# Attention keys in three chunks of 128 and a rest of 64, the rests of two head pairs on four quarters of the array

One core of one Trainium2 chip. The metric is the device time of one execution in microseconds (us). TensorE, VectorE, ScalarE and GpSimd are PE, DVE, ACT and POOL in the lines of the profile; PEld is the weight load of TensorE.

## The reference

```python
batch, n_heads, seq, head_dim = (8, 12, 448, 64)      # all fp32
def rmsnorm(x, g):
    return x / np.sqrt(np.mean(x * x, axis=-1, keepdims=True) + 1e-06) * g
q_n, k_n = rmsnorm(q, g_q), rmsnorm(k, g_k)
scores = (1 / sqrt(64)) * q_n @ k_n.T                  # per head, 448 x 448
attn = exp(scores - max) / (sum + 1e-9)
x = attn @ v                                           # to (3584, 768)
# then a SwiGLU feed-forward: rmsnorm(x), 768 -> 1536 (gate, value) -> 768
```

## The kernel before

Heads go in 48 pairs, six to a sequence. The 448 keys of a head are four chunks of 112. Per head pair: q and k are squared (ScalarE), reduced (VectorE) and turned into 1/rms (GpSimd power), q is multiplied by it (GpSimd), both are transposed on TensorE (`turn`) and copied out of PSUM. Scores have the keys on the output's partitions, so that k's 1/rms is the scale of the exp. Values and the sums of the exps accumulate over the chunks, a reciprocal follows, then the product x. While `direct(g)` holds (the first seven pairs) the sums are matmuls of ones over all exps; later GpSimd adds the exps first. In between run the matmuls of the feed-forward of the sequence before (`fill`). Up to about 300 us VectorE, ScalarE and GpSimd also convert the weights that arrive by DMA (`convert`).

```python
    ps_s, ps_m, ps_f = pool("c_ps_s", 4, space=PSUM), pool("c_ps_m", 1, space=PSUM), pool("c_ps_f", 3, space=PSUM)
    ...
    def turn(g, i):
        ...
        ps = (ps_m if todo else ps_f).tile([128, 512], F32, name="tr", tag="m" if todo else "f")
        for t in range(NT):                               # NT = 4, P = 112
            nc.tensor.transpose(ps[:, t * P:(t + 1) * P], src[:, t * 2 * D:(t + 1) * 2 * D], ident[0:P, 0:P])
        dst, flat = st["qkT", g][:, i, :], ps[:, 0:S]
        if i == 0:
            nc.scalar.activation(dst, flat, ACT.Copy, scale=gqk[:, 0:1])
        else:
            nc.vector.tensor_copy(dst, flat)

    def score(g, cs):
        ...
        for c in cs:
            for j in range(2):                            # j: head of the pair
                r = slice(j * D, (j + 1) * D)
                ps = sc[c, j] = ps_s.tile([128, 512], F32, name="sc", tag="s")
                nc.tensor.matmul(ps[0:P, 0:S], lhsT=qkT[r, 1, c * P:(c + 1) * P], rhs=qkT[r, 0, :], start=True, stop=True)
        ...                                               # exps; then add(): GpSimd, two adds after chunks 0 and 1, four after 2 and 3

    def values(g):
        vt = st["v", g]
        av = st["av", g] = ps_m.tile([128, 512], F32, name="av", tag="m")
        for c in range(NT):
            for j in range(2):
                nc.tensor.matmul(av[j * D:(j + 1) * D, 0:S], lhsT=vt[:, j, c, :], rhs=st["e", g, c, j],
                                 start=(c == 0), stop=(c == NT - 1))

    def sums(g):
        ...                                               # den: ones x exps
        rd = tmp.tile([128, S], F32, name="rd", tag="rd", bufs=1)
        if direct(g):
            nc.vector.reciprocal(rd, den[:, 0:S])
        ...
        nc.vector.tensor_tensor(x, av[:, 0:S], rd, ALU.mult)
        ...
            after(1 if soon else 3, lambda: nc.scalar.activation(rd, x, ACT.Square))
            after(1 if soon else 4, lambda: (nc.gpsimd.tensor_tensor(ss, ss, rd, ALU.add), ...))
    ...
        if g <= NPAIR:                                    # one head pair of the first stage (convert() cut)
            pe(lambda: score(g, (0, 1)))
            pe(lambda: turn(g + 1, 0)); pe(lambda: turn(g + 1, 1))
            pe(lambda: values(g - 1))
            pe(lambda: sums(g - 1))
            pe(lambda: score(g, (2, 3)))
```

Line numbers in the profiles are those of each kernel's own source. In the kernel before, scores are L476, values L501, sums L512, transposes L461; in the changed kernel scores are L532, values L579, sums L592, transposes L515 and L518, the quarters L556 (scores), L562 (values) and L567 (sums).

Of the kernel before, what the change touches and what calls it, by code (L numbers as in the profile page):

```python
# [20 lines left out]
NT, P = 4, 112  # L21
NPAIR = H // 2
# [312 lines left out]
def safe_scores(  # L335
# [28 lines left out]
    e_pool, tmp, y_pool = pool("c_e", 12), pool("c_tmp", 1), pool("c_y", 2)  # L364
# [25 lines left out]

    def load_pair(g):
        if g >= NG:
            return
        b, hp = divmod(g, NPAIR)
        hs = slice(2 * hp, 2 * hp + 2)
        qk = st["qk", g] = qk_pool.tile([P, 2, 2 * NT * D], F32, name="qk")
        nc.sync.dma_start(out=qk[:, 0].rearrange("p (h n) -> p h n", h=2), in_=q[b, hs].rearrange("h (p t) d -> p h (t d)", t=NT))

        for h in range(2):
            nc.sync.dma_start(out=qk[:, 1].rearrange("p (t h d) -> p h t d", h=2, d=D)[:, h],  # L400
                              in_=k[b, 2 * hp + h].rearrange("(p t) d -> p t d", t=NT))

    def load_v(g):
        if g >= NG:
            return
        b, hp = divmod(g, NPAIR)
        vt = st["v", g] = v_pool.tile([P, 2, NT, D], F32, name="vt")
        nc.sync.dma_start(out=vt.rearrange("p h t d -> p h (t d)"),
                          in_=v[b, 2 * hp:2 * hp + 2].rearrange("h (p t) d -> p h (t d)", t=NT))
# [5 lines left out]
    def squares(g, i):  # L415

        if g >= NG:
            return
        n = 2 * NT
        if i == 0:  # L420
            st["ms", g] = small.tile([P, 2 * n], F32, name="ms")
        ms = st["ms", g]
        sq = tmp.tile([P, n * D], F32, name="sq", tag="sq", bufs=2)
        nc.scalar.activation(sq, st["qk", g][:, i], ACT.Square)  # L424

        def reduce():
            nc.vector.tensor_reduce(out=ms[:, i * n:(i + 1) * n], in_=sq.rearrange("p (n d) -> p n d", d=D), axis=AX_X, op=ALU.add)  # L427

        after(1, reduce)
        if g <= 1:  # L430

            after(1, lambda: rms_qk(g, slice(i * n, (i + 1) * n)))
            if i == 0:
                after(1, lambda: norm_q(g))
        elif i == 1:
            after(2, lambda: rms_qk(g))
            after(2, lambda: norm_q(g))

    def rms_qk(g, cols=slice(0, 4 * NT)):
        ms = st["ms", g][:, cols]  # L440
        nc.gpsimd.tensor_scalar(ms, ms, 1.0 / D, 1e-6, ALU.mult, ALU.add)
        if ("rs", g) not in st:
            st["rs", g] = small.tile([P, 4 * NT], F32, name="rs")
        nc.gpsimd.tensor_tensor(st["rs", g][:, cols], ms, mhalf[0:P, cols], ALU.pow)  # L444

    def norm_q(g):
        qn = st["qn", g] = qn_pool.tile([P, 2 * NT * D], F32, name="qn")
        nc.gpsimd.tensor_tensor(
            qn.rearrange("p (t h d) -> p h t d", h=2, d=D), st["qk", g][:, 0].rearrange("p (h t d) -> p h t d", h=2, d=D),
            st["rs", g][:, 0:2 * NT].rearrange("p (h t) -> p h t", h=2).unsqueeze(3).to_broadcast([P, 2, NT, D]), ALU.mult)  # L450

    def turn(g, i):

        if g >= NG:
            return
        if ("qkT", g) not in st:
            st["qkT", g] = qkT_pool.tile([128, 2, S], F32, name="qkT")
        src = st.pop(("qn", g)) if i == 0 else st["qk", g][:, 1]
        ps = (ps_m if todo else ps_f).tile([128, 512], F32, name="tr", tag="m" if todo else "f")
        for t in range(NT):  # L460
            nc.tensor.transpose(ps[:, t * P:(t + 1) * P], src[:, t * 2 * D:(t + 1) * 2 * D], ident[0:P, 0:P])  # L461
        dst, flat = st["qkT", g][:, i, :], ps[:, 0:S]
        if i == 0:
            nc.scalar.activation(dst, flat, ACT.Copy, scale=gqk[:, 0:1])
        else:
            nc.vector.tensor_copy(dst, flat)  # L466

    def score(g, cs):

        qkT, rs = st["qkT", g], st["rs", g]  # L470
        sc = {}
        for c in cs:
            for j in range(2):
                r = slice(j * D, (j + 1) * D)
                ps = sc[c, j] = ps_s.tile([128, 512], F32, name="sc", tag="s")
                nc.tensor.matmul(ps[0:P, 0:S], lhsT=qkT[r, 1, c * P:(c + 1) * P], rhs=qkT[r, 0, :], start=True, stop=True)  # L476
        for (c, j), ps in sc.items():
            e = st["e", g, c, j] = e_pool.tile([P, S], F32, name="e")
            n = 2 * NT + c * 2 + j
            nc.scalar.activation(e, ps[0:P, 0:S], ACT.Exp, scale=rs[:, n:n + 1])  # L480

        def add():
            for j in range(2):
                if cs[0] == 0:
                    es = st["es", g, j] = tmp.tile([P, S], F32, name="es", tag="es", bufs=4)
                    nc.gpsimd.tensor_tensor(es, st["e", g, 0, j], st["e", g, 1, j], ALU.add)  # L486
                else:
                    es = st["es", g, j]
                    for c in cs:
                        nc.gpsimd.tensor_tensor(es, es, st["e", g, c, j], ALU.add)  # L490

        if not direct(g):
            after(4 if g == NPAIR + 1 else 1, add)

    def values(g):

        vt = st["v", g]
        av = st["av", g] = ps_m.tile([128, 512], F32, name="av", tag="m")
        for c in range(NT):
            for j in range(2):  # L500
                nc.tensor.matmul(av[j * D:(j + 1) * D, 0:S], lhsT=vt[:, j, c, :], rhs=st["e", g, c, j],  # L501
                                 start=(c == 0), stop=(c == NT - 1))

    def sums(g):
# [3 lines left out]
        den = (ps_f if direct(g) else ps_s).tile([128, 512], F32, name="den", tag="f" if direct(g) else "s")  # L508
        terms = [[st["e", g, c, j] for j in range(2)] for c in range(NT)] if direct(g) else [[st["es", g, j] for j in range(2)]]
        for i, pair in enumerate(terms):  # L510
            for j, term in enumerate(pair):
                nc.tensor.matmul(den[j * D:(j + 1) * D, 0:S], lhsT=ones[0:P, :], rhs=term,  # L512
                                 start=(i == 0), stop=(i == len(terms) - 1))
# [20 lines left out]
        for c in range(NT):  # L534
            for j in range(2):
                st.pop(("e", g, c, j))
# [370 lines left out]
    def store(b, n, i, y):  # L907
        row0 = at = b * S + i * 128 - 64 * (b % 2)
        while at < row0 + 128:
            seq, col = divmod(at, S)  # L910
            t, p = divmod(col, P)
            m = min(P - p, row0 + 128 - at)
            rows = out[seq * S:(seq + 1) * S, n * HALF:(n + 1) * HALF].rearrange("(p t) n -> t p n", t=NT)[t, p:p + m, :]
            nc.sync.dma_start(out=rows, in_=y[at - row0:at - row0 + m, :])
            at += m
# [175 lines left out]
    for g in range(2):  # L1091
        load_pair(g)
# [6 lines left out]
    mhalf = const.tile([128, 4 * NT], F32, name="mhalf")  # L1099
# [3 lines left out]
    for a in range(2):  # L1103
        rows = slice(a * D, (a + 1) * D)
        nc.scalar.dma_start(out=gq[rows, :], in_=g_q.rearrange("(p o) -> p o", o=1))
        nc.scalar.dma_start(out=gk[rows, :], in_=g_k.rearrange("(p o) -> p o", o=1))
    load_v(0)
    load_pair(2)
# [26 lines left out]


    squares(0, 0)
    warm(9)
# [7 lines left out]
    pe(lambda: turn(0, 0))  # L1146
    squares(2, 0)
    squares(2, 1)
    for g in range(NG + 1):
        b, hp = divmod(g, NPAIR)  # L1150
        if g:
            load_pair(g + 3)
        if g == 0:
            pe(lambda: score(0, (0, 1)))
            pe(lambda: score(0, (2, 3)))
# [9 lines left out]
        if g <= NPAIR:  # L1165
            pe(lambda: score(g, (0, 1)))
            squares(g + 2, 0)
            squares(g + 2, 1)
            convert()
            if g == 1:  # L1170
                pe(lambda: values(0))
            pe(lambda: turn(g + 1, 0))
            pe(lambda: turn(g + 1, 1))
            if g > 1:
                pe(lambda: values(g - 1))
            load_v(g + 2)
            convert()
            pe(lambda: sums(g - 1))
            pe(lambda: score(g, (2, 3)))
            convert()  # L1180
            if g == 2:
                bound()
            continue

        if g < NG:
            pe(lambda: score(g, (0, 1)))
        pe(lambda: values(g - 1))
        load_v(g + 2)
        if g == NPAIR + 1:
            pe(lambda: rms_x(0))  # L1190
            pe(lambda: score(g, (2, 3)))
# [4 lines left out]
        elif g < NG:  # L1196
            pe(lambda: score(g, (2, 3)))
        if hp:
# [3 lines left out]
            pe(lambda: turn(g + 1, 0))  # L1202
            fill()
# [55 lines left out]
```

## Time and profile before

| kernel before | |
|---|---|
| time, median of 3 runs | 1626.95 us (1626.43 to 1628.05) |
| span of the profiled execution, mean granted clock | 1625.3 us, 0.999 |
| TensorE busy | 99% |
| VectorE, ScalarE, GpSimd busy | 54%, 31%, 39% |

Busy shares are means over 1625 us.

### The profile page before, as it was taken

What the parts mean: (1) busy time and instruction counts of PE and PEld (TensorE: products, weight loads), DVE (VectorE), ACT (ScalarE), POOL (GpSimd) and SP (SyncE); (2) the same over time, 40 slices, a digit from 0 to 9 for tenths busy, and PEclk for the clock granted to TensorE, in tenths of its full rate; (3) what the DMA queues carried; (4) which work ended last, traced back from release to release, by engine and by line L of the source; (5) the groups of instructions that cost most, each with busy time, mean ns of one, the idle gap of its engine ahead of it and who ended that gap; (6) DMA issues with size and microseconds to landing.
All of it is one profiled execution on the core that took longest, in us unless ns stands there. A gap on an engine that the chain in (4) does not pass through costs nothing.

```text
span 1625.3 us, 21571 instructions
## 1 busy us (share of the span) xinstructions
PE 1608.9 (99%) x7376; PEld 1139.7 (70%) x7376; DVE 871.2 (54%) x1425; ACT 500.3 (31%) x975; POOL 632.2 (39%) x569
## 2 busy tenths in 40 slices
PE   8999999999999999999999999999999999999998
PEld 4444445678855888568865788658786588969974
DVE  6989898487842555335572354624565234433431
ACT  7856563232222332232232222322332123100110
POOL 7777776343523434244334323434343223100000
PEclk9999999999999999999999999999999999999999
DMA  8756674666855555565544655466454453557651
GB/s 223 208 176 200 183 219 134 217 222 200 267 183 154 164 154 156 166 197 154 155 120 131 201 155 147 120 215 194 130 163 132 147 176 108 152 182 239 175 148 45
DMA packets 249036, 276.83 MB, mean 170 GB/s; under 512 B 66644, under 2 KB 245844, under 8 KB 248916
## 3 DMA queue, kind: packets, MB, share of 16 engines
q1 hardware_dynamic: 248596, 275.34, 56.7%
q8 instruction: 61, 1.00, 0.3%
q14 instruction: 59, 0.48, 0.1%
q10 hardware_dynamic: 320, 0.00, 0.0%
HBM read 235.93 MB, written 39.32 MB: 169 GB/s over the span
## 4 chain that ended last, share of the span: by engine, by line
PE 91%; DVE 5%; DMA 2%; ACT 1%; issue 0%; POOL 0%; SPq 0%; DVEq 0%; ACTq 0%; POOLq 0%
PE ff L797 41%; PE ff L991 21%; PE sc L476 9%; PE av L501 9%; PE den L512 3%; PE ff L892 3%; PE ff L1022 2%; PE tr L461 2%; DVE top L646 1%; DVE top L645 1%; DVE rd L520 1%; DVE top L644 1%; DMA raw<-in_moe_w_out_dram 0%; ACT e L480 0%; PE rb L558 0%; DMA raw<-in_moe_w_val_dram 0%
## 5 line engine op out<-in xcount | busy, mean ns | idle before, releaser
L797 PE MATMUL ff<-x,w 128*128 128x224 f32 x1770 | 359.3, 353 | 0.8 <-DVE u L809 0.8
L797 PEld LDWEIGHTS ff<-x,w 128*128 128x128 f32 x1770 | 332.2, 190 | 9.8 <-issue 6.7
L797 PE MATMUL ff<-xs,w 128*128 128x224 f32 x1326 | 272.3, 353 | 0.4 <-DVE cc L809 0.4
L480 ACT ACTIVATE e<-sc,rs 112x448 f32<-112x448 f32 x384 | 212.1, 638 | 190.2 <-PE sc L476 185.2
L486 POOL TENSOR_TENSOR es<-e 112x448 f32<-112x448 f32 x82 | 95.3, 1184 | 436.1 <-ACT e L480 436.0
L797 PEld LDWEIGHTS ff<-xs,w 128*128 128x128 f32 x1326 | 248.6, 190 | 6.1 <-issue 5.3
L490 POOL TENSOR_TENSOR es<-es,e 112x448 f32<-112x448 f32 x164 | 185.9, 1144 | 85.4 <-ACT e L480 78.9
L991 PE MATMUL ff<-w,h 128*128 128x384 f32 x600 | 203.4, 488 | 0.0
L520 DVE RECIPROCAL rd<-rd 128x448 f32<-128x448 f32 x41 | 121.1, 2953 | 135.9 <-ACT rd L519 135.9
L476 PE MATMUL sc<-qkT 64*112 64x448 f32 x768 | 176.7, 562 | 1.6 <-DVE qkT L466 0.8
L991 PEld LDWEIGHTS ff<-w,h 128*128 128x128 f32 x600 | 112.3, 190 | 78.6 <-issue 4.7
L501 PE MATMUL av<-e,vt 112*64 112x448 f32 x768 | 154.9, 545 | 0.0
L444 POOL TENSOR_TENSOR rs<-ms,mhalf 112x16 f32<-112x16 f32 (+1 forms) x50 | 143.7, 2874 | 4.2
L476 PEld LDWEIGHTS sc<-qkT 64*112 64x112 f32 x768 | 68.8, 172 | 93.2 <-issue 69.5
L991 PE MATMUL ff<-w,so 128*128 128x384 f32 x338 | 116.7, 488 | 2.0 <-DVE y L952 2.0
L501 PEld LDWEIGHTS av<-e,vt 112*64 112x64 f32 x768 | 50.8, 136 | 95.8 <-issue 73.9
L1022 PE MATMUL ff<-x,w 128*128 128x448 f32 x288 | 112.0, 542 | 0.0
L809 DVE TENSOR_TENSOR cc<-ff,u 128x448 f32<-128x448 f32 x84 | 52.3, 623 | 93.3 <-PE ff L797 93.0
L991 PEld LDWEIGHTS ff<-w,so 128*128 128x128 f32 x338 | 63.2, 190 | 46.5 <-DVE y L952 3.9
L427 DVE TENSOR_REDUCE ms<-sq 112x8 f32<-112x512 f32 x96 | 61.3, 678 | 52.0 <-ACT sq L424 51.7
L682 POOL TENSOR_TENSOR w<-top,raw 128x384 int32<-128x384 int32 x72 | 78.0, 1097 | 28.3 <-DVE top L646 13.4
L1022 PEld LDWEIGHTS ff<-x,w 128*128 128x128 f32 x288 | 53.3, 190 | 50.9 <-issue 49.0
(104 smaller groups left out, 1676.2 us busy)
## 6 DMA issues: line engine op xcount, KB each, us to landing
w<-kept SPq DMA_DIRECT2D x480, 192.0 KB, 3.2
w<-kept_o SPq DMA_DIRECT2D x290, 192.0 KB, 2.8
kept<-w SPq DMA_DIRECT2D x94, 192.0 KB, 3.7
top<-kept SPq DMA_DIRECT2D x72, 192.0 KB, 3.0
qk<-in_q_dram SPq DMA_DIRECT2D x48, 224.0 KB, 3.6
qk<-in_k_dram SPq DMA_DIRECT2D x96, 112.0 KB, 3.5
vt<-in_v_dram SPq DMA_DIRECT2D x48, 224.0 KB, 2.8
raw<-in_moe_w_gate_dram SPq DMA_DIRECT2D x24, 384.0 KB, 4.7
```

The source lines that it names most:

```text
L427: nc.vector.tensor_reduce(out=ms[:, i * n:(i + 1) * n], in_=sq.rearrange("p (n d) -> p n d", d=D), axis=AX_X, op=ALU.add)
L444: nc.gpsimd.tensor_tensor(st["rs", g][:, cols], ms, mhalf[0:P, cols], ALU.pow)
L476: nc.tensor.matmul(ps[0:P, 0:S], lhsT=qkT[r, 1, c * P:(c + 1) * P], rhs=qkT[r, 0, :], start=True, stop=True)
L480: nc.scalar.activation(e, ps[0:P, 0:S], ACT.Exp, scale=rs[:, n:n + 1])
L486: nc.gpsimd.tensor_tensor(es, st["e", g, 0, j], st["e", g, 1, j], ALU.add)
L490: nc.gpsimd.tensor_tensor(es, es, st["e", g, c, j], ALU.add)
L501: nc.tensor.matmul(av[j * D:(j + 1) * D, 0:S], lhsT=vt[:, j, c, :], rhs=st["e", g, c, j], start=(c == 0), stop=(c == NT - 1))
L520: nc.vector.reciprocal(rd, rd)
L682: nc.gpsimd.tensor_tensor(data(key).bitcast(I32), top, lo, ALU.add)
L797: nc.tensor.matmul(bank[:, w * HT:(w + 1) * HT], lhsT=wt[:, c * 128:(c + 1) * 128], rhs=x[:, c, :], start=onto is None and w == c == 0, st ...
L991: nc.tensor.matmul(ps, lhsT=a, rhs=data(("wo", b, name, c)), start=first and c == 0, stop=c == NFP - 1, skip_group_check=True)
L1022: nc.tensor.matmul(bank[w][:, 0:S], lhsT=data(key)[:, c * 128:(c + 1) * 128], rhs=st["x", 0, half][:, c, :], start=half == c == 0, stop=ha ...
```

## The change

The intent: four chunks of 112 rows use only 112 of the array's 128 rows or columns. Three chunks of 128 and a rest of 64 have less to do: the rest scores of two heads need 64 x 64 of the array each, and so do the rest values, so all four can stand on the four quarters at once. The rests of a sequence's six pairs are loaded, normalized and (q with k) transposed together. The core of the diff:

```diff
+    def norm_rests(b, lo, hi):
+        nc.scalar.activation(sq, rest, ACT.Square)
+        after(1, lambda: nc.vector.tensor_reduce(out=ms, in_=sq, axis=AX_X, op=ALU.add))
+        def rms():
+            nc.gpsimd.tensor_scalar(ms, ms, 1.0 / D, 1e-6, ALU.mult, ALU.add)
+            nc.gpsimd.tensor_tensor(rq, ms[0:D], half[0:D], ALU.pow)
+            nc.gpsimd.tensor_tensor(rest[0:D], rest[0:D], rq.unsqueeze(3).to_broadcast([D, n, 2, D]), ALU.mult)
+            for place in range(2):
+                nc.gpsimd.tensor_tensor(st["rr", b][own(place), lo:hi], ms[own(1), :, place], half[own(1), :, place], ALU.pow)
...
     def turn(g, i):
-        for t in range(NT):
-            nc.tensor.transpose(ps[:, t * P:(t + 1) * P], ...)
+        for t in range(NK):                                   # NK = 3
+            nc.tensor.transpose(ps[:, t * 128:(t + 1) * 128], ...)
         if i == 0:
+            nc.tensor.transpose(ps[:, NK * 128:], st["rest", b][:, hp].rearrange("p h d -> p (h d)"), ident)
+            nc.scalar.activation(dst[:, 0, :], ps[:, 0:S], ACT.Copy, scale=gqk[:, 0:1])
+            nc.vector.tensor_copy(dst[:, 1, LAST], ps[:, S:])
         else:
-            nc.vector.tensor_copy(dst, flat)
+            nc.vector.tensor_copy(dst[:, 1, FULL], ps[:, FULL])
...
         def add():                                            # once per pair, after the last chunk
+                nc.gpsimd.tensor_tensor(es, st["e", g, 0, j], st["e", g, 1, j], ALU.add)
+                nc.gpsimd.tensor_tensor(es, es, st["e", g, 2, j], ALU.add)
+                nc.gpsimd.tensor_tensor(es[r], es[r], rest[r], ALU.add)
...
+    def rests(g):                       # quarters: this pair's rest scores, the last pair's rest values (and sums)
+            for r in (own(0), own(1)):
+                nc.tensor.matmul(ps[r, 0:S], lhsT=qkT[r, 1, LAST], rhs=qkT[r, 0, :], start=True, stop=True)
+            for j in range(2):
+                nc.tensor.matmul(av[own(j), 0:S], lhsT=vr[across(j)], rhs=e[across(j)], start=True, stop=False, ...)
...
         if g <= NPAIR:
-            pe(lambda: score(g, (0, 1)))
-            pe(lambda: turn(g + 1, 0)); pe(lambda: turn(g + 1, 1))
-            pe(lambda: values(g - 1)); pe(lambda: sums(g - 1)); pe(lambda: score(g, (2, 3)))
+            pe(lambda: score(g, (0,)))
+            pe(lambda: turn(g + 1, 0)); some_rests(g); pe(lambda: turn(g + 1, 1))
+            pe(lambda: rests(g)); pe(lambda: values(g - 1))
+            pe(lambda: score(g, (1,))); pe(lambda: sums(g - 1)); pe(lambda: score(g, (2,)))
```

(In the later stages, `rests(g)` stands ahead of the first scores.)

## The prediction

> **What bounds the kernel now.** I read the page's busy shares first, then the costliest groups, then the timeline of one head pair in the long middle stage, and last the windows of the first 300 us.
>
> ```profile
> PE 1608.9 (99%) x7376; PEld 1139.7 (70%) x7376; DVE 871.2 (54%) x1425; ACT 500.3 (31%) x975; POOL 632.2 (39%) x569
> PE 91%; DVE 5%; DMA 2%; ACT 1%; issue 0%; POOL 0%; SPq 0%; DVEq 0%; ACTq 0%; POOLq 0%
> L476 PE MATMUL sc<-qkT 64*112 64x448 f32 x768 | 176.7, 562 | 1.6 <-DVE qkT L466 0.8
> L501 PE MATMUL av<-e,vt 112*64 112x448 f32 x768 | 154.9, 545 | 0.0
> ```
>
> TensorE is never idle to speak of, and the chain that ended last is TensorE for 91% of the span. So time comes only from fewer TensorE steps, and only where TensorE really holds the pace. Scores (L476) and values (L501) are a fifth of it. Each has 768 records for 48 x 8 = 384 matmuls: an fp32 matmul leaves two records. The timeline of TensorE around one pair of heads:
>
> ```profile
> 619.86 2.43 PE L797 MATMUL ff<-xs,w 128*128 128x224 f32 x12
> 622.23 1.76 PE L476 MATMUL sc<-qkT 64*112 64x448 f32 x8
> 623.92 3.23 PE L501 MATMUL av<-e,vt 112*64 112x448 f32 x16
> 626.98 0.92 PE L512 MATMUL den<-es,ones 112*64 112x448 f32 x4
> 627.83 1.78 PE L476 MATMUL sc<-qkT 64*112 64x448 f32 x8
> 629.54 2.54 PE L797 MATMUL ff<-x,w 128*128 128x224 f32 x12
> ```
>
> Take differences of starts, because the ends are modelled. Values: 626.98 - 623.92 = 3.06 us for 16 records, 0.191 each. A full-array matmul of the same 448 columns needs twice that:
>
> ```profile
> 122.11 7.03 PE L1022 MATMUL ff<-x,w 128*128 128x448 f32 x18
> 128.98 0.55 PE L461 MATMUL tr<-ident,qn 112*128 112x112 f32 x4
> ```
>
> (128.98 - 122.11) / 18 = 0.38 us. So the two heads' matmuls run side by side, on two halves of the array, and what counts is the number of **pair steps**: two records per matmul, 0.375 us apart, 0.75 us per pair. The weight loads show the 0.375 directly, two at a time:
>
> ```profile
> 622.70 0.18 PEld L476 LDWEIGHTS sc<-qkT 64*112 64x112 f32 x2 [0.20 <-issue]
> 623.07 0.18 PEld L476 LDWEIGHTS sc<-qkT 64*112 64x112 f32 x2 [0.20 <-issue]
> ```
>
> A head pair is then 2 + 4 + 1 + 2 = 9 pair steps = 6.75 us. It took 629.54 - 622.23 = 7.31 us; the 0.56 over falls on three stretches (1.69 - 1.50 = 0.19, 3.91 - 3.75 = 0.16, 1.71 - 1.50 = 0.21): each switch between halves by rows (scores), halves by columns (values, sums) and the whole array costs about 0.19 us.
>
> The first stage is another case:
>
> ```profile
> 36.40:47.70 11.30, 11.30 (x58) 4.68 (x58) 10.79 (x17) 9.06 (x18) 5.97 (x8) 1.00 0.76 222
> 59.00:70.30 11.30, 11.30 (x60) 4.68 (x58) 11.06 (x15) 9.05 (x18) 8.50 (x8) 1.00 0.73 214
> 150.00:200.00 50.00, 48.59 (x160) 23.41 (x158) 45.42 (x63) 25.52 (x53) 37.81 (x34) 1.00 0.61 181
> ```
>
> The columns are stretch and length, then busy time of TensorE, weight loads, VectorE, ScalarE, GpSimd. VectorE, which converts the weights, is 95 to 98% busy up to 82 us and 91% at 150 to 200 us, and GpSimd is at 53 to 76%. What TensorE saves there can turn into waiting.
>
> **What the Trainium skill says.** "TensorEngine Tiling (Array Packing)", Key Properties: tiles work independently, each with its own weight loads and matmuls, but "Changing tiling mode (not just tile) drains the TensorE". The trace agrees with both: pairs at 0.375 us a step, and 0.16 to 0.21 us lost per switch. "TensorE: Matmul & The Clock Gate", Part 3 (Packing small matmuls): a packed group spans one matmul plus about 4 ns per tile, measured there up to 16 tiles in bf16. Here the second of a pair starts 7 ns after the first; no group of four runs in this kernel, so four is carried over. The same page, LDWEIGHTS: a load's time goes with its columns, not its rows. The trace agrees (scores 64x112 about 172 ns, values 112x64 about 137 ns), so filling 128 partitions rather than 112 costs the values nothing. "PSUM — Partial Sum Buffer", collisions: it quotes that different row tiles are not able to write one bank at the same time. The trace of before cannot test that, since its row halves write different banks.
>
> **The change part by part.**
>
> *Removed:* per head pair, of the four pair steps of scores and of values one each (4 chunks of 112 become 3 of 128). Minus 1.50 us.
>
> *Added:* one group of four quarter matmuls: this head pair's two rest scores (rows and columns of the same half) and the last pair's two rest values (crossed). If four run as two did: 0.75 us. The heads lie crossed in the tiles for just this.
>
> *Switches:* before: scores, values + sums, scores: three stretches. After: quarters, scores, values + sums, scores: four. Plus 0.19 us.
>
> *Sum after the first stage:* 1 + 1 + 3 + 1 + 2 = 8 pair steps, 6.00 us, plus 0.75 of switches = 6.75 against 7.31: **minus 0.56 us per head pair**.
>
> *Transposes:* 8 of 112 columns become 7 of 128, the rests of q and k of a pair in one. Four took 613.04 - 612.65 = 0.39 us in the middle stage, 0.097 each; by columns 0.11 each, so 7 x 0.11 = 0.77 against 0.78. Nothing.
>
> *Sums while direct* (first seven head pairs): four pair steps stay four, since the rests' sums sit on quarters that the rest values already hold and queue behind them. There too it is 12 steps to 11.
>
> *ScalarE:* exps per pair 8 to 7. ScalarE is 31% busy and gives nothing, except in the first stage: eight score matmuls there run on end against four banks, and take 40.56 - 36.32 = 4.24 us rather than 3.00 + 0.19. The new order spreads them, so up to 1.0 us of waiting per pair could go as well. TensorE's need per pair there: 11.3 - 0.75 - 1.0 + three more switches (0.57) = about 10.1 us.
>
> *VectorE:* reductions 112x512 at 678 ns become 128x384, about 0.52 by size: minus 0.3 per pair; an extra small copy plus 0.1; two rest reductions per sequence, plus 0.17 per pair. No relief: an estimated 10.9 us per pair in the first stage. Hence I expect 10.9 there and not 10.1: six pairs x 0.4 = 2.4 us.
>
> *GpSimd:* the power is 2.98 us for 16 columns and 1.65 for 8, so 0.166 per column: 12 columns 2.3, minus 0.7 per pair. Rests per sequence: twice (0.2 + 1.3 + 0.9 + 2 x 0.83) = 8 us, plus 1.35 per pair. Six adds per pair stay six (the last two on half the partitions take as long). At 39% busy this lies beside other work, except at the start, where the first head pair now also needs its rest normalized and ScalarE issues four loads first. GpSimd is 10.75 of 12 us busy at 13 to 25 us. I put the start at plus 2.5 us.
>
> *Loads:* some 256-byte pieces more for rests, twelve per 31 us stretch at most; DMA is half idle. Hidden.
>
> *Total:* head pairs 13 to 47, after the conversions: 35 x 0.56 = 19.6 us. Pairs 8 to 12, where VectorE is at 90% and the chain runs through it: half of 5 x 0.56, 1.4. Pair 7: 0.5. First stage 2.4 less 2.5. Sum 21.4 us: 1626.9 - 21.4 = about **1605.5 us**, 1.3% faster.
>
> **The rivals.**
>
> *Four quarters run as two pairs* (weights, row inputs or the bank rule keep them apart). Then there are still nine pair steps, plus one switch: 47 x 0.19 = 9 us slower, plus the start: about 1638. Against it: row halves and column halves both already run side by side at full rate, with different data streamed to each. For it: no trace here shows four. 10%.
>
> *TensorE bound everywhere, VectorE no limit.* First stage 6 x 1.2 = 7 us, pairs 7 to 12 in full, start free: 19.6 + 3.4 + 7 = 30 us, 1597. VectorE's 95 to 98% speaks against; that its conversion steps are stretched (L644's row means 649 ns, but 0.28 us occurs alone) and could shrink speaks for. 15%.
>
> *The start and first stage become GpSimd bound.* Rest work there comes three times (4 us each) and the first pairs wait for it: plus 6 to 8 us, 1612. 20%.
>
> **Range and chances.** The bulk, 19.6 us, rests on one mechanism that either holds or not; around it the first 240 us are worth from plus 8 to minus 10. Range 1596 to 1618. Over 2% faster means under 1594.4, beyond the best rival's sum: 8%. Over 2% slower (1659) is out of reach even for the pairs rival: 1%. Within 2%: 91%.
>
> **What would show it.** Right: the weight loads of the rest scores and rest values come four at a time, and the next scores start 0.90 to 0.98 us after the group's first matmul; a middle head pair takes about 6.75 us from first score to next projection; TensorE stays at 99%; VectorE is above 95% in the first 80 us. Wrong: the group takes 1.6 us (pairs rival); gaps on TensorE ahead of transposes with GpSimd as releaser (third rival); the first direct pairs at 10.1 us each (second). A wait ahead of the rest values on the one PSUM buffer they share with the transposes would also break the sum.

## The result, and the profile after

The changed kernel took 1640.81 us (median of 4 runs, 1637.92 to 1642.06), the kernel before 1627.50 us (4 runs, 1626.43 to 1628.49) in the same rounds. The ratio is 1.0079, 95% interval 1.0062 to 1.0097: slower by 0.8%. The predicted 1605.5 us, and its range, were missed.

The busy shares of the page and the chain that ended last, of the changed kernel:

```profile
PE 1595.4 (98%) x7328; PEld 1125.6 (69%) x7328; DVE 873.6 (53%) x1490; ACT 476.4 (29%) x944; POOL 672.0 (41%) x706
PE 83%; DVE 9%; POOL 3%; DMA 2%; issue 1%; ACT 1%; SPq 0%; DVEq 0%; POOLq 0%; ACTq 0%
```

TensorE has 13.5 us less to do, and the span is 10.8 us longer (1636.1 against 1625.3). TensorE's part of the chain fell from 91% to 83%; VectorE and GpSimd took it over.

The timeline of TensorE in the long middle stage, changed kernel (start, length, engine, line, output from inputs, shape, count):

```profile
614.09 0.59 PE L556 MATMUL sc<-qkT 64*64 64x448 f32 x2
614.10 0.59 PE L562 MATMUL av<-e,vr 64*64 64x448 f32 x2
614.51 0.54 PE L556 MATMUL sc<-qkT 64*64 64x448 f32 x2
614.53 0.54 PE L562 MATMUL av<-e,vr 64*64 64x448 f32 x2
615.00 1.02 PE L532 MATMUL sc<-qkT 64*128 64x448 f32 x4
615.95 2.48 PE L579 MATMUL av<-e,vt 128*64 128x448 f32 x12
618.26 0.92 PE L592 MATMUL den<-es,ones 128*64 128x448 f32 x4
619.11 1.80 PE L532 MATMUL sc<-qkT 64*128 64x448 f32 x8
620.84 1.40 PE L878 MATMUL ff<-x,w 128*128 128x224 f32 x6
```

Four quarters do run side by side: the group takes 615.00 - 614.09 = 0.91 us, and the head pair 620.84 - 614.09 = 6.75 us, to the hundredth what was predicted. So the mechanism holds, and the loss lies elsewhere. To find it I took from both traces the start of each head pair's first full values matmul (`av<-e,vt`) and subtracted before from after. This **lag** is the measure for the rest of this document (in us):

```
pair        0     3     5     6     7     9    10    11    12    14    15    18    46   end
lag      8.60  8.47 10.49 12.36 11.01 11.33 17.11 19.56 23.31 22.11 25.40 28.00 10.99 10.86
```

From pair 18 on the lag falls by (28.00 - 10.99) / 28 = 0.61 us a pair, as the mechanism says (0.56 predicted). But by then it has grown to 28 us, in steps: 8.6 at the start, 2.5 in the first stage, 12.3 at pairs 10 to 12, 5.9 at pairs 15 to 18. Each step shows a wait.

**Start.** Timeline of GpSimd and TensorE, changed kernel:

```profile
10.96 0.48 PE L518 MATMUL tr<-ident,rest 128*128 128x128 f32 x1 [0.77 <-POOL rest L456]
12.43 1.76 PE L556 MATMUL sc<-qkT 64*64 64x448 f32 x4 [0.98 <-DVE qkT L520]
...
19.70 0.60 POOL L456 TENSOR_TENSOR rest<-rest,rq 64x256 f32<-64x256 f32 x1
20.36 0.33 PE L518 MATMUL tr<-ident,rest 128*128 128x128 f32 x1 [1.59 <-POOL rest L456]
```

The first scores start at 12.43 us (before 9.91), and TensorE waits twice for the rests' normalization on GpSimd. The windows of before, then of after (the column after the five engines' busy times is the granted clock):

```profile
8.00:12.00 4.00, 2.58 (x13) 1.25 (x14) 1.80 (x3) 2.58 (x5) 3.67 (x5) 1.00 0.99 244
12.00:16.00 4.00, 3.28 (x16) 1.63 (x15) 0.62 (x1) 4.00 (x9) 3.63 (x5) 1.00 1.15 311
```

```profile
8.00:12.00 4.00, 1.27 (x4) 0.57 (x4) 1.43 (x5) 2.23 (x5) 3.51 (x8) 0.70 1.10 224
12.00:16.00 4.00, 3.58 (x10) 1.36 (x12) 2.67 (x6) 2.10 (x5) 3.58 (x6) 0.50 1.04 336
```

GpSimd, the fifth, is as full in both (3.5 to 3.7 of 4 us), so each piece of rest work delays the rest of its queue. And TensorE, which is also busy for less of the time before (1.27 of 4 us against 2.58), is granted only half its clock at 12 to 16 us.

**First stage.** Windows of the changed kernel, the same stretches as in the prediction:

```profile
36.40:47.70 11.30, 11.10 (x57) 3.94 (x55) 10.27 (x16) 8.49 (x18) 8.24 (x9) 1.00 0.94 244
59.00:70.30 11.30, 10.21 (x48) 3.57 (x47) 8.62 (x16) 8.68 (x19) 10.59 (x12) 1.00 0.55 167
```

VectorE, which was to be the bound, has fallen to 91% and 76%; GpSimd in the second stretch has risen to 94%. Pairs 1 to 3 still take 11.3 us each. And the group of four does not form there: at pairs 2 to 4 the values' quarters start 1.2 to 1.3 us after the scores' quarters (0.01 us in the middle stage, see above), so that they take two steps and not one, and the step that was to be saved is not. The experiments below look for the reason. From pair 4 on TensorE waits for GpSimd ahead of its transposes, as in the third rival (timeline, changed kernel):

```profile
70.04 0.55 PE L515 MATMUL tr<-ident,qn 128*128 128x128 f32 x3 [0.73 <-POOL qn L500]
83.24 0.55 PE L515 MATMUL tr<-ident,qn 128*128 128x128 f32 x3 [1.56 <-POOL qn L500]
```

**Pair 10.** Timeline of the changed kernel:

```profile
182.97 1.97 POOL L458 TENSOR_TENSOR rr<-msr,mhalf 64x3 f32<-64x3 f32 x2
185.02 4.15 POOL L763 TENSOR_TENSOR w<-top,raw 128x384 int32<-128x384 int32 x4
...
189.89 0.55 ACT L719 ACTIVATE top<-raw 128x384 f32<-128x384 f32 x1 [1.85 <-DMA raw<-in_moe_w_gate_dram]
190.78 0.61 ACT L572 ACTIVATE e<-sc,rr 128x448 f32<-128x448 f32 x1
191.44 3.87 PE L532 MATMUL sc<-qkT 64*128 64x448 f32 x8 [5.08 <-ACT e L572]
```

Read upwards: TensorE waits 5.08 us for the exp that frees its scores' bank; the exp stands in ScalarE's queue behind a conversion that waits for its DMA; that DMA could start only when its buffer was free, which the last conversion step (`w`, GpSimd) frees; and four of those steps stood behind the power of the next sequence's rests. In the kernel before the same place cost 1.41 us. Directly after, eight scores take 3.87 us where they usually take 1.8: the window 190 to 220 us has a granted clock of 0.89 (before 1.00).

**Pairs 11 and 12.** Timeline of the changed kernel:

```profile
237.16 0.55 PE L515 MATMUL tr<-ident,qk 128*128 128x128 f32 x3 [1.49 <-DVE qkT L520]
...
265.03 0.55 PE L515 MATMUL tr<-ident,qk 128*128 128x128 f32 x3 [2.29 <-DVE qkT L520]
```

L520 is a new copy, 128x64, 0.21 us: k's rests out of q's transposed bank. In this stage both transposes use the single bank of `ps_m`, so k's wait until this copy is done, and it stands in VectorE's queue behind conversions.

**Pairs 15 to 18.** Timeline of the changed kernel, with VectorE and GpSimd:

```profile
357.61 1.34 POOL L544 TENSOR_TENSOR es<-es,e 128x448 f32<-128x448 f32 x1
358.41 2.37 DVE L835 TENSOR_TENSOR w<-w,w 128x384 f32<-128x384 f32 x2
...
362.64 0.54 DVE L835 TENSOR_TENSOR w<-w,w 128x384 f32<-128x384 f32 x1
366.52 0.65 PE L878 MATMUL ff<-x,w 128*128 128x224 f32 x2 [1.94 <-ACT p L911]
```

The six adds of a pair now run in one piece on GpSimd (352.6 to 361.8 us with the sum of squares). Beside them a 128x384 add on VectorE takes 1.2 us in the mean, after them 0.54; GpSimd's adds go from 1.14 to 1.34 us themselves. The Trainium skill, "SBUF — State Buffer", Who interferes with whom, says that a VectorE instruction with two inputs in SBUF contends with a GpSimd instruction that reads SBUF, and that the contention is an exclusive lock. The trace fits that: each of the five slowed VectorE adds between 355.7 and 362.2 us ends 0.41 or 0.42 us after the end of a GpSimd instruction. VectorE falls behind, and TensorE waits (in the line shown by way of ScalarE, which had waited 2.14 us for a VectorE reduction).

### The profile page after: what moved, and what is told of

Its sections match the earlier page's. It is cut to its first block, busy times and chain, and to the rows that moved or that the text cites. A ratio compares the mean times of both kernels' runs of the same rounds, so it can differ in the third digit from the quotient of the medians.

```text
span 1636.1 us, 21612 instructions
## 1 busy us (share of the span) xinstructions
PE 1595.4 (98%) x7328; PEld 1125.6 (69%) x7328; DVE 873.6 (53%) x1490; ACT 476.4 (29%) x944; POOL 672.0 (41%) x706
## 4 chain that ended last, share of the span: by engine, by line
PE 83%; DVE 9%; POOL 3%; DMA 2%; issue 1%; ACT 1%; SPq 0%; DVEq 0%; POOLq 0%; ACTq 0%
PE ff L878 38%; PE ff L1076 21%; PE av L579 6%; PE sc L532 6%; PE ff L973 3%; PE den L592 2%; PE sc L556 2%; PE ff L1107 2%; DVE rd L600 2%; PE tr L515 1%; DVE top L725 1%; DVE top L726 1%; DVE top L727 1%; DVE w L835 1%; POOL rs L495 1%
## 5 line engine op out<-in xcount | busy, mean ns | idle before, releaser
L878 PEld LDWEIGHTS ff<-x,w 128*128 128x128 f32 x1770 | 333.5, 191 | 13.5 <-issue 6.5
L543 POOL TENSOR_TENSOR es<-e 128x448 f32<-128x448 f32 x82 | 94.0, 1146 | 543.5 <-ACT e L536 540.2
L536 ACT ACTIVATE e<-sc,rs 128x448 f32<-128x448 f32 x288 | 162.0, 633 | 42.4 <-PE sc L532 40.8
L532 PE MATMUL sc<-qkT 64*128 64x448 f32 x576 | 140.8, 583 | 7.5 <-ACT e L572 6.0
L579 PE MATMUL av<-e,vt 128*64 128x448 f32 x576 | 119.0, 548 | 0.0
L532 PEld LDWEIGHTS sc<-qkT 64*128 64x128 f32 x576 | 54.6, 189 | 90.5 <-issue 68.7
L495 POOL TENSOR_TENSOR rs<-ms,mhalf 128x12 f32<-128x12 f32 (+1 forms) x50 | 113.2, 2263 | 4.2
L544 POOL TENSOR_TENSOR es<-es,e 128x448 f32<-128x448 f32 x82 | 94.4, 1152 | 7.8 <-ACT e L536 1.5
L545 POOL TENSOR_TENSOR es<-es,e 64x448 f32<-64x448 f32 x82 | 94.6, 1154 | 6.4
L579 PEld LDWEIGHTS av<-e,vt 128*64 128x64 f32 x576 | 37.2, 137 | 76.9 <-issue 73.4
```

The source lines that it names most:

```text
L495: nc.gpsimd.tensor_tensor(st["rs", g][:, cols], ms, mhalf[:, cols], ALU.pow)
L532: nc.tensor.matmul(ps[:, 0:S], lhsT=qkT[r, 1, c * 128:(c + 1) * 128], rhs=qkT[r, 0, :], start=True, stop=True)
L536: nc.scalar.activation(e, ps[:, 0:S], ACT.Exp, scale=rs[:, n:n + 1])
L543: nc.gpsimd.tensor_tensor(es, st["e", g, 0, j], st["e", g, 1, j], ALU.add)
L544: nc.gpsimd.tensor_tensor(es, es, st["e", g, 2, j], ALU.add)
L545: nc.gpsimd.tensor_tensor(es[r], es[r], rest[r], ALU.add)
```

## The experiments

**Theory A**: the rests' normalization on GpSimd, some 4 us in one piece, delays what stands behind it. **Theory B**: the small copy on VectorE holds the one bank. **Theory C**: the run of six adds slows VectorE. Rivals are in the expectations. (The expectations use older letters: the adds are their theory B, the clock at the start their C, the small copy their D.) Ratios are to the kernel before in the same rounds; the changed kernel's own is 1.0079. All kernels but the first gave a correct result.

### norest: later sequences' rests not normalized (wrong result)

```diff
 def norm_rests(b, lo, hi):
-    if b >= B: return
+    if b: st["rr", b] = st["rr", 0]; return
```

> Wrong on purpose: the rests of sequences 1 to 7 are loaded but not normalized (no squares, reductions or GpSimd work for them; the factors of sequence 0 are used again). Theory A, that the block of five GpSimd instructions per half sequence (about 5 us) stands ahead of the weight joins and the q normalization and so delays TensorE between 60 and 460 us: the lag behind the kernel before, which grew from 8.5 us at head pair 3 to 28 us at head pair 18, stops growing, and the total falls by 15 to 20 us to about 1622. Theory B, that the six adds in one run on GpSimd are to blame: most of the lag stays, 1632 or more. Under both the start keeps its 8.6 us.

Measured: 1629.8 us, ratio 1.0003 [0.9986, 1.0019]; this lies between the two forecasts. By the ratios this work costs 0.76%, some 12 us (the rests' squares on ScalarE and reductions on VectorE are in that too; the run onepow below changes GpSimd alone). (A profile is one execution; norest's was its slowest, 1633.3 us, and the changed kernel's its fastest, 1637.9, so the ends of the lags differ by 4.6 us only.) The lag shows places: at pair 5 8.6 instead of 10.5, at 10 15.7 instead of 17.1, at 15 20.9 instead of 25.4. In pairs 10 to 12 most of the loss stays (21.9 at pair 12): theory A is true and is not enough. At pair 10 TensorE still waits 3.2 us for the same exp (5.08 in the changed kernel) with no such rest work on GpSimd at all, and ScalarE again waits for a DMA of gate weights, 3.4 us. So the rests account for under 2 us of the chain read above, and what makes the rest of it longer than the 1.41 us of before stays open. (Its waits for GpSimd in the first stage are gone, but after the wait ahead of pair 7 the clock was halved for some 3 us, so the lag at pair 6, 12.1, is no better there.)

### spread: the rests' GpSimd steps one at a time, between other work

```diff
-  four GpSimd instructions in one go
+  b > 0: each in a later slot, after(1), after(2), after(3), after(4)
```

> The four long GpSimd instructions of the rest normalization are issued one TensorE step apart instead of in a row (sequences 1 to 7), the work is the same. Theory A in the form that the unbroken block delays what stands behind it in the queue: half of the lag or more goes, about 1628 to 1632. Theory A in the form that GpSimd has too much to do in all: no change, 1638 to 1641. Theory B: no change.

Measured: 1637.1 us, ratio 1.0054 [1.0038, 1.0071]. It is 2.8 us worse than the changed kernel by pair 6 (lag 15.2), 1.2 better at pair 12 and 2.9 better at pair 15 (22.5). Neither forecast was met. The size of the piece is about 4 of the 12 us of theory A; that the rest is the sum of the work, above all in the first stage, where GpSimd has little room in any order, is my reading and no run shows it alone.

### adds: two adds of each head after chunk 1, one after chunk 2

```diff
-  rests(g), score(g, (0,)) ... score(g, (1, 2)), then 3 adds per head
+  rests(g), score(g, (0, 1)), 2 adds per head ... score(g, (2,)), 1 add per head
```

> Scores of chunks 0 and 1 together ahead of the values, chunk 2 after the sums, and so four of the six GpSimd adds of a head pair run early and two late, where the change had all six late in one run. Theory B (bunched adds slow VectorE and delay the weight joins): the waits on VectorE drains at head pairs 15 to 18 (about 4 us) go and part of those at pairs 10 to 12, together 6 to 12 us, about 1630. Theory A: 1637 to 1641.

Measured: 1634.9 us, ratio 1.0039 [1.0022, 1.0055]. The waits of pairs 15 to 18 are gone (lag 27.8 at pair 15, 25.8 at 18, falling all the way; all TensorE's waits between 340 and 480 us come to 1.0 us instead of 6.4): theory C holds. The edit has a price of its own: the rest scores and two chunks need five banks of a ring of four at once, and while ScalarE converts, TensorE waits 4.5 and 4.2 us for exps (lag 23.0 at pair 9, 27.6 at 10).

### warm: 22 in place of 3 dummy matmuls at the start

```diff
-    warm(3)
+    warm(22)
```

> 22 dummy matmuls instead of 3 ahead of the first transposes of q, which fill TensorE's idle time from 7 to 9.4 us. Theory C, that TensorE's idle time at the start lets its clock fall to half and that this costs 3 to 4 us of the 8.6 lost there: first scores no longer 0.8 us apart but 0.375, lag at the first values 4.5 to 6 us, total about 1637. Rival: the start is set by the chain through the rests' loads and GpSimd, and TensorE's clock does not matter there: lag at the first values stays over 8 us, total 1640.

Measured: 1641.5 us, ratio 1.0078 [1.0061, 1.0095]; lag 10.5 at pair 0. The clock is 1.0 from 8 to 24 us and 0.57 at 24 to 28 us. But the dummies stood in the way themselves: they ran until q's transposes started at 13.72 us (9.41 in the changed kernel), and the first scores came at 15.30 us (12.43). From first scores to first values it took 13.0 us, against 13.9. So these dummies do not shorten the start; what the clock costs there, the run cannot tell.

### acopy: the small copy on ScalarE

```diff
-            nc.vector.tensor_copy(dst[:, 1, LAST], ps[:, S:])
+            nc.scalar.copy(dst[:, 1, LAST], ps[:, S:])
```

> The small copy of a pair's k rests out of the bank of the turned q is given to ScalarE, which empties the rest of that bank anyway, instead of VectorE. Theory D: TensorE's waits of 1.5 to 2.3 us ahead of the transposes of k (head pairs 11, 12 and 18), named with VectorE's small copy as releaser, come from this copy alone, because both turns share one bank with the rest values and VectorE is deep in conversions there. Then these waits go, with the half clock that follows one of them: 5 to 7 us, total about 1634. Rival: VectorE is simply late in this stage, and the wait moves to the next thing that needs it (the big copy of k, or the bank of the values): under 2 us, 1639 to 1641.

Measured: 1630.3 us, ratio 1.0012 [0.9996, 1.0029]: one 0.21 us copy was worth 10.6 us, more than the 5 to 7 expected. No transposes wait for L520 any more, and the lag stands at 18.5 at pairs 11 and 12 instead of 19.6 and 23.3, and ends at 2.45. At the start this profile is 2 us ahead (6.65 at pair 0), but not by the copy: dvelight below has the same copy and 8.8 at pair 0, and by pair 6 the lead is gone (13.4 against 12.4). (Its windows give a clock of 1.00 from 8 us on, but its trace has no clock record before 16.7 us, and its first four quarters take 1.76 us as in the changed kernel, where the clock is 0.50; in warm they take 0.97.) The wait at pair 10 stays:

```profile
192.26 3.87 PE L532 MATMUL sc<-qkT 64*128 64x448 f32 x8 [4.98 <-ACT e L572]
```

### onepow: one power for q's and k's rests on all partitions, then copies

```diff
-            nc.gpsimd.tensor_tensor(rq, ms[0:D], half[0:D], ALU.pow)
+            nc.gpsimd.tensor_tensor(rq, ms, half, ALU.pow)
...
-                nc.gpsimd.tensor_tensor(st["rr", b][own(place), lo:hi], ms[...], half[...], ALU.pow)
+                nc.gpsimd.tensor_copy(st["rr", b][own(place), lo:hi], rq[own(1), :, place])
```

> The rest normalization takes one power over all 128 partitions and two small copies instead of three powers: its block on GpSimd falls from about 5 us to about 3. If the block's length is what costs (theory A, 5 to 8 us by the run without any rest normalization, which took 11 us off with 0 us of block), about half of that comes back: 4 to 6 us, 1635 to 1637; most of it at head pairs 4 to 6, where the lag grew 3.9 us. If not: 1640.

Measured: 1633.4 us, ratio 1.0029 [1.0012, 1.0046]: 7 us from 2.9 us less GpSimd work a sequence (the powers and copies for `rr` sum to 7.4 instead of 30.2 us over the kernel). Lag 9.1 at pair 5, 13.5 at pair 10, 19.2 at pair 12 (10.5, 17.1 and 23.3 in the changed kernel). Theory A again, here with a correct result.

### start2: the first rests' loads off ScalarE, the first k squares early

```diff
-    load_rests(0, nc.scalar)
+    load_rests(0, nc.gpsimd, 0, 1)      # first pair's rests
...
+    load_rests(0, nc.sync, 1, NPAIR)    # the others, later
...
     squares(0, 0)
+    squares(0, 1)
     norm_rests(0, 0, 1)
```

> Start only: the first pair's rests are loaded alone by the GpSimd queue, the other five pairs' after pair 1 by the sync queue, the gains by ScalarE as in the kernel before; ScalarE squares k ahead of the rests. Theory: the 8.6 us at the start are the chain four load issues on ScalarE, rests landing at 8.7 us, their normalization on GpSimd, first transposes; the dummy matmuls did not help since TensorE only waits there. First scores then come at 10.5 to 11 us instead of 12.4, lag at the first values 4 to 6 us instead of 8.6, total 1636 to 1638. If GpSimd's own queue of work from 12 to 20 us sets the first values (it was 90% busy there before the change too): lag 7 us or more, total 1639 or more.

Measured: 1640.6 us, ratio 1.0075 [1.0058, 1.0092]; first scores at 12.00 instead of 12.43 us, lag 8.3 at pair 0. A miss, as the second forecast has it: ScalarE's queue was not what held the start alone. TensorE still waits 1.6 us for pair 1's rest on GpSimd.

### combo: acopy, onepow and start2, and the adds split from pair 13 on

> The three above together, and from head pair 13 on the score chunks 0 and 1 ahead of the values, so that four of six adds run early (the part of the earlier run of that kind that helped, without the part that hurt while weights are converted). If the causes are separate, the gains add: 6 + 5 + 3 + 6 = about 20 us, total about 1621, faster than the kernel before by 0.4%. If they are one chain through which the latest piece always shows, less than 12 us: 1629 or more.

The edit is that of the three runs together; the adds are split as in the run "adds" only for g > 12, where no conversions are left. Measured: 1618.0 us, ratio 0.9938 [0.9921, 0.9955]: the change, mended, is faster than the kernel before. The separate gains against the changed kernel in ratio are 0.67 (acopy), 0.50 (onepow), 0.04 (start2) and 0.40 (adds) per cent, 1.61 together, and the combination gains 1.41: they nearly add up, as separate causes would. (Each ratio is known to some 0.17% either way, and the adds are split in fewer pairs than in the run "adds", so this supports it and does not prove it.) Lag 5.3 at pair 0, 8.3 at 10, 11.3 at 12, 7.6 at 18, -9.9 at the end.

What was still open was the first stage: 11.3 us a pair in every kernel so far.

### dvelight: the large copy of k on ScalarE too while direct

```diff
-            nc.vector.tensor_copy(dst[:, 1, FULL], ps[:, FULL])
+            (nc.scalar.copy if direct(g - 1) else nc.vector.tensor_copy)(dst[:, 1, FULL], ps[:, FULL])
```

(and the small copy as in acopy)

> Correct result. As the run that moved the small copy of k's rests to ScalarE, and in the first stage (pairs 0 to 6) the large copy of k's transposed chunks (128x384) moves from VectorE to ScalarE too. It asks why the first stage kept 11.3 us a pair although its TensorE work became less. Theory (VectorE is the bound of pairs 1 to 3, busy over 90%): the lag behind the kernel before falls by 0.3 to 0.5 us a pair from pair 1 to pair 4 where the small-copy run's stayed at 6.4 us, and the end comes about 1.5 to 2 us earlier, near 1628.5. Rival (GpSimd, busy 9.8 to 10.4 us of each 11 from pair 4 on, is the bound, or ScalarE becomes it): the lag stays at 6.4 us or grows, and the jump of some 7 us from pair 4 to pair 6 stays as it was; the time is 1630 or more.

Measured: 1629.3 us, ratio 1.0008 [0.9991, 1.0025]. The lag does not move: 8.55, 8.53, 8.58, 8.63 at pairs 1 to 4. VectorE has 0.5 to 0.7 us less to do than in the changed kernel in each of the stretches 28 to 39, 39 to 51 and 51 to 62 us. That changes nothing, so **VectorE's load is not what sets 11.3 us there**. The timeline of the changed kernel shows what does:

```profile
46.98 0.97 PE L556 MATMUL sc<-qkT 64*64 64x448 f32 x4
...
48.24 0.97 PE L562 MATMUL av<-e,vr 64*64 64x448 f32 x4 [0.29 <-DVE x L607]
...
55.85 2.96 DVE L596 RECIPROCAL rd<-den 128x448 f32<-128x448 f32 x1 [0.90 <-PE den L592]
...
58.84 0.62 DVE L607 TENSOR_TENSOR x<-av,rd 128x448 f32<-128x448 f32 x1
...
59.61 0.59 PE L562 MATMUL av<-e,vr 64*64 64x448 f32 x2 [0.36 <-DVE x L607]
```

It is a loop around the one bank of the values. The rest values open the bank; then come on TensorE rest sums, values, scores, sums; then VectorE's reciprocal and product, which closes the bank; then the next rest values. From 48.24 to 59.61 that is 11.37 us, of which 3.6 are the two VectorE steps. The wait itself is only 0.3 us, but it also tears the group apart: the scores' quarters, ready earlier, run alone at 46.98 us, the values' quarters at 48.24, and 49.02 - 46.98 = 2.04 us go where four together take some 0.8 (0.81 in combo4 below, 42.64 to 43.45 us). In the kernel before the bank was opened later, by the values themselves. **Theory D**: this latency loop sets the stage's pace; its rival is the engines' load.

### combo2: at pair 7 the scores of the first chunk ahead of the rests

```diff
-        pe(lambda: (rests(g), score(g, first) if g < NG else None))
+        if g == NPAIR + 1:
+            pe(lambda: (score(g, first), rests(g)))
+        else:
+            pe(lambda: (rests(g), score(g, first) if g < NG else None))
```

(on top of combo)

> Correct result. The run of four repairs together, with one more: at pair 7, the first after the direct stage, the chunk scores are issued ahead of the rests' quarters, which wait for the one PSUM bank of the values. Theory (that wait, about 2 us in the changed kernel near 95 us, stands on the path, because TensorE is the bound there): pair 7's lag falls by 1 to 2 us and the time from 1618 to about 1616.5. Rival (the time comes back within three pairs because the exps or the conversions set the pace there): the lag at pair 10 is the same 8.3 us within 0.5, and the time 1618 within 1.

Measured: 1615.9 us, ratio 0.9928 [0.9911, 0.9944]. Lag 5.4 at pair 7 (combo 6.5), 7.1 at pair 10 (8.3): 1.0 us gained and kept, in the scores' place beside the same loop's wait.

### swap and combo3: in the first stage the sums ahead of the values

```diff
             pe(lambda: rests(g))
-            pe(lambda: values(g - 1))
+            pe(lambda: rds.append(sums(g - 1)))              # sums and reciprocal
...
             pe(lambda: score(g, (1,)))
-            pe(lambda: sums(g - 1))
-            pe(lambda: score(g, (2,)))
+            pe(lambda: values(g - 1))
+            pe(lambda: (products(g - 1, rds.pop()), score(g, (2,))))
```

(swap on the changed kernel, combo3 on combo2)

> Correct result; only the order in the first stage (pairs 0 to 5) is changed: a pair's sums with their reciprocal come ahead of its values instead of after them. It asks why the first stage kept 11.3 us a pair, now that VectorE as the bound has fallen. Theory (a loop around the one PSUM bank of the values: rest values 0.77, rest sums 0.88, values 2.4, scores 0.95, sums 2.4, reciprocal 2.96, product 0.62 and the hops between them make 11.37 us, the period seen): with the reciprocal beside the values the waits of the rest values for VectorE's x go, pairs 1 to 3 take 10.6 us (my count of their TensorE rows) to 11.0 instead of 11.37, so the lag falls from 8.4 at pair 1 to between 6.5 and 7.5 at pair 3. Rival (conversions on VectorE and GpSimd set the pace all the same): lag 8.4 to 8.6 at pair 3. At pairs 4 to 6 GpSimd is busy over 9.7 of each 11 us, so I expect it to take back most of what is won: 11 to 13 us at pair 6, and a time of 1639 to 1641.

> Correct result. The five repairs together with the order of the first stage changed as in the run beside it. Theory of the loop: lag at pair 3 about 4 instead of 5.0 us; at pair 6 5 to 6.8 us, since GpSimd has more room here (rest normalization shortened), and the time 1614 to 1616. Rival: lag at pair 3 stays 5.0, time 1616 or more.

Measured: swap 1653.6 us, ratio 1.0150 [1.0133, 1.0167]; combo3 1628.9 us, ratio 1.0006 [0.9989, 1.0022]. Both far off. In combo3 one pair, from one group of quarters to the next, took 52.93 - 42.88 = 10.05 us, with no wait on TensorE; after it VectorE's reciprocal waited. The waits of VectorE between 40 and 90 us of combo3 (waited for; us in total, times, longest):

```profile
DVE rd L603 <- POOL ss L626: 12.2, 3, 4.4
```

The reciprocal writes `rd`, of which there is one, and which is also the scratch from which GpSimd adds the last pair's squares. Earlier in the pair the reciprocal meets that add, and the add waits in GpSimd's queue. Taking one wait away had uncovered another.

### swap2 and combo4: the squares in an idle buffer instead

```diff
+        sq = tmp.tile([128, S], F32, name="es", tag="es", bufs=4) if direct(g) else rd
-            ... nc.scalar.activation(rd, x, ACT.Square)
-            ... nc.gpsimd.tensor_tensor(ss, ss, rd, ALU.add)
+            ... nc.scalar.activation(sq, x, ACT.Square)
+            ... nc.gpsimd.tensor_tensor(ss, ss, sq, ALU.add)
```

(I found no room for a second `rd` in SBUF, which no run shows; `es` is idle in this stage)

> Correct result. As the run with sums ahead of values, and the squares of the products go into an idle buffer instead of the reciprocal's. Theory of the loop: VectorE's reciprocals no longer wait for GpSimd's sum of squares, no rest values wait for VectorE's product, and pairs 1 to 3 take 10.1 to 10.7 us each instead of 11.37; at pair 6 (where the order of the marks is the same again) the lag is below the changed kernel's 12.4 us unless GpSimd, the bound of pairs 4 to 6 by its busy time, takes it back: I expect 10 to 12.5 there and 1637 to 1641 in all. Rival (the conversions on VectorE and GpSimd set the pace): periods stay at 11.3 and other waits come in place of these.

> Correct result. The five repairs with sums ahead of values and the squares in an idle buffer. Theory of the loop: pairs 1 to 3 take 10.1 to 10.7 us, the lag at pair 6 falls from 6.8 to between 3.5 and 6, and the time to between 1612 and 1615. Rival: lag at pair 6 6.5 to 8, time 1615 to 1618.

Measured: combo4 1613.1 us, ratio 0.9904 [0.9888, 0.9921], the fastest kernel; lag 3.6 at pair 6 instead of 6.8 in combo2, as theory D expected. The periods were met in part: from one group of quarters to the next, pairs 1, 2 and 3 took 11.39, 10.05 and 10.76 us (combo2 10.96, 11.21 and 11.30). Its windows in the first stage:

```profile
36.40:47.70 11.30, 11.30 (x63) 4.11 (x61) 11.02 (x18) 7.81 (x17) 6.61 (x8) 1.00 0.98 253
59.00:70.30 11.30, 10.81 (x55) 4.14 (x55) 11.09 (x18) 7.84 (x16) 10.59 (x13) 1.00 0.62 193
```

With the loop cut at pairs 1 to 3, VectorE is 98% busy and TensorE 100 and 96%: now those two fill the stage, and it wins 3.2 us and no more. swap2 took 1640.6 us, ratio 1.0075 [1.0058, 1.0092]: as the changed kernel. Its reciprocals no longer wait for GpSimd either, but VectorE waits 9.6 us in three places for the copy that shares q's bank (L520 behind ScalarE's L519), GpSimd holds the transposes for 1.16 us, and the lag at pair 6 is 15.1, above the 10 to 12.5 that I expected. Nor is the loop cut there: the rest values wait 2.9 us in four places for VectorE's product (0.9 in three in the changed kernel), pair 2 takes 10.25 us, and pair 3 11.29 again. That is closer to the rival's forecast, other waits in place of these. So theory D is shown for single pairs and on top of the five repairs; what the loop alone costs in the changed kernel stays open.

The lags of the runs, from the traces (us; swap, combo3, swap2 and combo4 have another order up to pair 5, so that their marks are comparable from pair 6 on):

```
pair        0      3      6      9     10     12     15     18     46    end
after    8.60   8.47  12.36  11.33  17.11  23.31  25.40  28.00  10.99  10.86
norest   8.74   8.50  12.11  11.04  15.72  21.94  20.90  23.51   6.50   6.24
spread   9.01   8.78  15.15  14.14  16.42  22.09  22.50  25.15   8.14   8.05
adds     8.86   8.63  16.45  22.96  27.57  29.16  27.82  25.83   9.30   8.29
acopy    6.65   6.41  13.43  12.25  17.67  18.45  18.65  19.71   2.71   2.45
onepow   8.17   7.93  10.94   9.87  13.52  19.18  21.27  23.87   6.86   6.69
combo    5.33   5.09   7.81   5.74   8.33  11.27   9.76   7.64  -8.89  -9.92
combo2   5.24   5.01   6.79   4.85   7.12   9.20   7.68   5.56 -10.97 -11.98
swap2                 15.11  14.72  19.98  26.40  28.49  31.09  14.08  13.85
combo4                 3.55   1.64   4.14   7.11   5.59   3.46 -13.06 -13.97
```

## Why the prediction was wrong

*The group of quarters: right.* 0.91 us, within the 0.90 to 0.98 named; the pairs rival is out.

*Minus 0.56 us per head pair: right, in fewer pairs.* It came to 0.61, but from pair 18 on only: 28 pairs and 17.0 us, where the sum had 35 pairs and 19.6.

*Pairs 13 to 18, in that sum with minus 3.4 us: wrong.* The lag grew by 5.3 from pair 13 (22.7) to 18. The step said that six adds stay six. They do; but they became one run of six, and beside it VectorE's adds take over twice as long. The run "adds" shows it.

*Pairs 7 to 12, minus 1.9 us: wrong, the largest miss.* The lag went from 11.0 to 23.3. The sum allowed for half the gain being lost to VectorE; it did not ask what else hangs on the new work. Two things did: "an extra small copy plus 0.1" was small all the same (0.21 us) and placed wrongly, in a full queue while it held a bank that TensorE needed (acopy), and the rests' GpSimd work stood ahead of a conversion that frees a DMA's buffer (onepow, norest; at pair 10 this is under 2 of the 5.08 us, and the rest of that wait stays open). "At 39% busy this lies beside other work" was the failing sentence: the sizes were right (the four rest operations on GpSimd sum to 70.5 us, 8.8 a sequence, against my 8), but they come as blocks of 4 to 5 us in a stretch where GpSimd is some 76% busy.

*First stage, minus 2.4 us, VectorE as the bound: wrong.* It gained nothing, and VectorE was not its bound: dvelight took load from it without effect. The step "12 steps to 11" failed too: at pairs 2 to 4 the values' quarters came 1.2 to 1.3 us after the scores' quarters, so that it stayed 12. They waited in a loop around the one bank of the values, and from pair 4 on GpSimd came on top. With the loop cut single pairs took 10.05 us (combo3, combo4), near the 10.1 of TensorE's need, and on top of the other repairs 3.2 us were won; in the changed kernel alone the same edit left the rest values waiting and won nothing (swap2). The prediction named that bank in its last sentence as a way to break the sum, and gave it no number, though its parts (2.96 us of reciprocal among them) could have been added up beforehand. VectorE is as full as predicted (98%) only in combo4.

*Start, plus 2.5 us: a size off.* It was 8.6. The first scores came 2.5 us later, just the estimate; the second pair's rests then waited for GpSimd again, and the clock halved. My repairs took back 3.3 of it (combo). How the other 5.3 divide between ScalarE's and GpSimd's queues and the clock, no run settles.

*The rivals.* "Start and first stage GpSimd bound" came nearest in kind: it had plus 6 to 8 us, and the lag at pair 7 was 11.0. But its 1612 us kept the whole later gain; none of the three had a loss at 100 to 480 us. The pairs rival's 1638 us is the number nearest to the 1640.8 measured, but by luck: its mechanism is out, the group taking 0.91 us and not 1.6.

## What to carry to other kernels

When a change trims the bounding engine, list each small piece that it adds to other engines and ask what stands behind that piece in its queue and which single buffer it holds; the mean busy share answers neither. Here a 0.21 us copy cost 10 us and blocks of 4 to 5 us cost 7 to 12. Then walk the loops through single buffers and add up their latencies, because a shorter bound makes the next loop the pace: first this bank, then the reciprocal's scratch. And a mended version can be worth the work: the same idea with the pieces moved is 1.0% faster than the kernel before, where as written it was 0.8% slower.

## What the Trainium skill lacked or had wrong

- "TensorEngine Tiling (Array Packing)", Key Properties: says that changing the tiling mode drains TensorE, with no size. Here 0.16 to 0.21 us per switch (fp32, 448 columns); a group of four quarters with its switch takes 0.91 us.
- "PSUM — Partial Sum Buffer", on bank collisions: the rule quoted there, that different row tiles can't access one bank at the same time, is stricter than what ran here. Two rest matmuls from different row halves write one bank at the same time, on different partitions, 0.91 us for the group, with a correct result. (They lie in different column tiles too, which the same quote allows.) The page's own rule by quadrant agrees.
- "TensorE: Matmul & The Clock Gate", Part 1: names an idle window of about 3.4 us as what halves the clock. The wait of 5.08 us agrees with it: the eight scores after it took 3.87 us instead of 1.8. But in the changed kernel the clock was also halved shortly after waits of 2.29 us (up to 265.03 us; 0.66 in the window 265 to 270 us) and of 1.94 us (up to 366.52 us; 0.72 in the window 366 to 372 us). Here shorter waits were enough.
